# Cached attention decode on one core: K loaded and transposed in pairs of tiles

## The chip, the core and the metric

The kernel runs on one core of a Trainium2 chip. The core has five engines that run their own instruction streams and meet at semaphores: TensorE (PE, with its weight loads shown as PEld), VectorE (DVE), ScalarE (ACT), GpSimd (POOL) and SyncE (SP, which here only issues DMAs). Sixteen DMA engines move data between the device memory and the on-chip memory (SBUF, 128 partitions). The metric is the device time in microseconds of one execution; smaller is better. Before the change the median of three runs is 1311.87 us (1311.55 to 1312.01).

## What is computed

One decode step of a block with grouped-query attention over a long cache, and a gated unit beside it. There are 2 sequences, one new token each, width 512; 32 query heads share 8 key/value heads; the cache holds 32768 positions of 128 numbers per sequence and key/value head. Everything is float32.

```python
xn = _layernorm(x, axis=-1)
# attention
q = (xn @ wq) as 32 heads of 128
scores = einsum("bhqd,bhkd->bhqk", q, k_cache repeated 4 times) * (128 ** -0.5)
o = einsum("bhqk,bhkd->bhqd", softmax(scores), v_cache repeated 4 times)
s = o.reshape(2, 1, 4096) @ wo
# gated unit
gate, up = xn @ W_gate, xn @ W_up
g = silu((relu(gate) * up) @ W_down)
return x + s * g
```

K and V are 268 MB each. Together with `wq`, `wo` and the three matrices of the gated unit the kernel must read 564.7 MB. Each number of K and V is used by the four query heads of one group only.

## The kernel before

**Groups, tiles, steps.** A group is one sequence and one key/value head; there are 16 (`NG`), each with 32768 positions, cut into 4 tiles (`NU`) of 8192 positions (`TK`). A K tile is 4 MiB: 128 partitions x 64 positions x 128 numbers. There are 64 tiles (`NK`). A step `s` of the main loop (line 904) does the scores of tile `s` and, from step 4 on, the softmax weights of tile `s - 4`. At each odd step the values of two tiles, `s - 5` and `s - 4`, follow the scores on PE. Two tiles that share a stretch of 16384 positions are called a pair here: partition `p` holds 128 neighbouring positions of it, tile `2j` the first 64 of these, tile `2j + 1` the others (`rows_of`, line 400). So a tile of K loaded alone takes 32 KB in a row from every 64 KB, and a pair of V takes 64 KB in a row.

**Work of a step.** DVE transposes the K tile in four chunks of 128x2048 numbers, in blocks of 32x32 (`k_transpose`, line 663), from one of two K slots `kslot` into the tiles `kts` (five of them, so that the first chunk of an odd tile has its own). PE multiplies the transposed chunks with the current query `qcur` (`scores`, line 676). DVE copies the scores of the tile before out of PSUM and notes their maximum (`take_scores`), transposes weights (`take_weights`), and between them does the few small operations that a new group needs: at a step divisible by 4 the group's maximum is found, ACT takes the exponentials of its four tiles, and the group before the last is scaled and turned into a column of `ots` (`finish_group`, line 798; its last copy is ACT's). At the group's last step POOL copies the next group's query from `qt` to `qcur` (`take_query`, line 547). `qt` holds every group's query in a form with zeros around it.

**Loads.** All large loads are issued by SP, in program order, and SP waits at each one until the buffer is free. The lists `ahead` and `at` (lines 876 to 897) say at which step each is issued. Before the loop come `wq` (into `wide`), K tiles 0 and 1, then the two matrices of the gated unit (into `wide`, when the query projection has read it). At each step `s` up to 61 K tile `s + 2` is issued into the slot that tile `s` leaves; its wait is for DVE's transposes of tile `s`. At step 1 `W_down` follows, and at each odd step from 3 a pair of V (`load_vv`) goes into `wide`, 64 KB per partition, a single buffer: it waits until PE has done the values of the pair before.

**The end.** The last four V tiles go apart: tiles 60 and 61 one by one into the free K slots (`load_v`), tile 62 whole and tile 63 in two halves into `wide` (`load_apart`). The output weights `wo` come in eight blocks of 1 MiB, one for each key/value head: four into `kts` before the last V (`load_early`), four into a K slot after it (`load_late`), the very last block in three pieces. `project_near` multiplies blocks 0 to 6 with `ots` in one form and `project_far` block 7 in another that is shorter behind the last bytes; `END` is step 68.

**Loops.** DVE and PE run steps 4 to 63 as a hardware loop of 15 rounds of four steps, with semaphore values kept in registers (`looped` and `emit`); ACT, POOL and SP run straight code. `in_halves` shows a tile as two halves of four chunks, eight positions each.

Of the kernel before, what the change touches and what calls it, by code (L numbers as in the profile page):

```python
# [8 lines left out]
P = 128  # L9
Q = 32  # L10
NC = 4
NR = 16
TK = P * NC * NR
EARLY = 4
NEAR = 7
# [147 lines left out]
def decode_block_kernel(nc, x, kc, vc, wq, wo, wg, wu, wd, out):  # L163
# [17 lines left out]
    def sbuf(name, *shape, align=32):  # L181
        return nc.alloc_sbuf_tensor(name, list(shape), F32, align_bytes=align)[:]
# [23 lines left out]
    qd = sbuf("qd", P, REP, B, HKV)  # L206
    qt = sbuf("qt", P, B, HKV, 4, Q)
    qcur = sbuf("qcur", P, 4, Q)
# [20 lines left out]
    def dve(fn, r=(), w=()):  # L229
        pg.op("DVE", fn, r, w)  # L230
# [7 lines left out]
    def load(dst, src, sem, r=(), w=(), engine="SP"):  # L238
        pg.op(engine, lambda e: e.dma_start(dst, src), r, w, dma=sem)  # L239
# [54 lines left out]
    dve(lambda e: e.memset(zero, 0.0), w=["zero"])  # L294
    dve(lambda e: e.memset(qt, 0.0), w=["qt"])
    dve(lambda e: e.memset(heads, 0.0), w=["heads"])
# [99 lines left out]

    def load_k(t):
        load(kslot[t % 2], rows_of(kc, t, 1), f"k{t % 2}", w=[f"k{t % 2}"])

    def rows_of(src, t, n):  # L400
        b, hk = group(t // NU)
        lo = (t % NU) // 2 * 2 * TK
        rows = src[b, hk, lo : lo + 2 * TK, :]
        if n == 2:
            return rows.rearrange("(p r) d -> p (r d)", p=P)
        return rows.rearrange("(p i r) d -> i p (r d)", i=2, p=P)[t % 2]

    HALF = NC * NR * DH

    def place(t):  # L410
        if t in (NK - 4, NK - 3):
            return kslot[t % 2], [f"k{t % 2}"]
        half = wide[:, t % 2 * HALF : (t % 2 + 1) * HALF]
        return half, [f"wide{t % 2}"]

    def load_v(t):
        load(kslot[t % 2], rows_of(vc, t, 1), f"k{t % 2}", w=[f"k{t % 2}"])

    def load_vv(t):
        load(wide, rows_of(vc, t, 2), "v", w=["wide", "wide0", "wide1"])  # L420

    def load_apart(t):
        load(wide[:, :HALF], rows_of(vc, t, 1), "v_a", w=["wide0"])
        n = HALF // 2
        for h in range(2):
            load(
                wide[:, HALF + h * n : HALF + (h + 1) * n],
                rows_of(vc, t + 1, 1)[:, h * n : (h + 1) * n],
                f"v_b{h}",
                w=["wide1" if h == 0 else "wide1h"],  # L430
            )

    def in_halves(tokens):
        return tokens.rearrange("p (h c r d) -> p h c r d", h=2, c=NC, d=DH)

    wo_early = [kts[hk].rearrange("p (j d) -> p j d", j=4) for hk in range(EARLY)]
    late = HKV - EARLY
    WO, WOK = {}, {}

    def load_early():  # L440
        for hk in range(EARLY):
            WO[hk], WOK[hk] = wo_early[hk], [f"kts{hk}"]
            load(
                kts[hk],
                wo[hk * REP * DH : (hk + 1) * REP * DH, :].rearrange("(p j) d -> p (j d)", j=4),
                f"wo{hk}",
                w=[f"kts{hk}"],
            )

    def load_late():  # L450
        slot = kslot[(NK - 4) % 2]
        key = f"k{(NK - 4) % 2}"
        for hk in range(EARLY, HKV):
            i = hk - EARLY
            dst = slot[:, i * 4 * D : (i + 1) * 4 * D]
            WO[hk] = dst.rearrange("p (j d) -> p j d", j=4)
            here = wo[hk * REP * DH : (hk + 1) * REP * DH, :]
            rows = here.rearrange("(p j) d -> p (j d)", j=4)
            cuts = ((0, 4),) if hk < HKV - 1 else ((0, 2), (2, 3), (3, 4))
            WOK[hk] = {}  # L460
            for lo, hi in cuts:
                name = f"{key}_{hk}_{lo}"
                for j in range(lo, hi):
                    WOK[hk][j] = name
                load(
                    dst[:, lo * D : hi * D],
                    rows[:, lo * D : hi * D],
                    f"wo{hk}_{lo}",
                    r=(),
                    w=[key, name] if (hk, lo) == (EARLY, 0) else [name],  # L470
                )

    def project_q():
# [58 lines left out]
        )  # L532
        for kb in range(4):
            part = slice(Q * kb, Q * kb + Q)
            dve(
                lambda e, kb=kb, part=part: e.tensor_copy(  # L536
                    qt[part, :, :, :, kb * REP : (kb + 1) * REP].rearrange(
                        "p b k e h -> p (b k) e h"
                    ),
                    pq2[part, : 4 * nq].rearrange("p (e h g) -> p g e h", e=4, h=REP),  # L540
                ),
                ["pt1"],
                ["qt"],
            )
        take_query(0)

    def take_query(g):
        b, hk = group(g)
        pg.op("POOL", lambda e: e.tensor_copy(qcur, qt[:, b, hk]), ["qt"], ["qcur"])

# [109 lines left out]
    def turned(t, c):  # L660
        i = NC if c == 0 and t % 2 else c
        return kts[i], f"kts{i}"

    def k_transpose(t, c):
        src = kslot[t % 2]
        dst, key = turned(t, c)
        dve(
            lambda e: e.transpose(  # L668
                dst.rearrange("p (h n) -> p h n", h=2),
                in_halves(src)[:, :, c].rearrange("p h r d -> p h (r d)"),  # L670
            ),
            [f"k{t % 2}"],
            [key],
        )

    def scores(t):
        ps = ps_s[t % 2]

        def one(e, c):
            part = turned(t, c)[0].rearrange("p (r e k) -> p r e k", e=4, k=Q)  # L680
            return mm(ps[Q * c : Q * c + Q, :], qcur[:, e, :], part[:, :, e, :], e == 0, e == 3)
# [71 lines left out]
    def values(t):  # L753
        u = t % NU
        at_, keys = place(t)
# [12 lines left out]
        for h in range(2):  # L768
            held = keys if t < NK - 1 or h == 0 else ["wide1h"]
            pe(chain([one(r) for r in range(8 * h, 8 * h + 8)]), [f"wt{t % 2}", *held], ["o"])  # L770

# [26 lines left out]
    def finish_group(g):  # L798
# [15 lines left out]
        dve(lambda e: e.transpose(ot, ob), ["ob"], ["ot"])  # L814
        act(
            lambda e: e.copy(ots[:, hk, :, b * APART], ot.rearrange("p (j m) -> p j m", j=4)[:, :, 0]),
            ["ot"],
# [6 lines left out]
    def project_near(hks):  # L824
        for hk in hks:
            held = WOK[hk] if isinstance(WOK[hk], list) else [WOK[hk][0]]
            pe(
# [11 lines left out]
                ),  # L839
                [f"ots{hk}", *held],  # L840
                ["s0"],
# [45 lines left out]
    at(ahead, NK - 2, load_v, NK - 4)  # L887
    at(ahead, NK - 1, load_v, NK - 3)
    at(ahead, NK - 1, load_early)
    at(ahead, NK - 1, load_apart, NK - 2)  # L890
    at(ahead, NK + 1, load_late)
    at(extra, NK + 2, project_near, range(EARLY))
    at(extra, 1, mlp_gu, "g", 0)
    at(extra, 1, mlp_gu, "u", 1)
    at(extra, 3, mlp_vector)
    at(extra, 3, mlp_down)
    at(extra, 3, total)

    load_k(0)
    load_k(1)  # L900
    project_q()
    load_gu()

    for s in range(END + 1):
# [18 lines left out]
        if s == END:  # L923
            project_near(range(EARLY, EARLY + 1))
        if done is not None:
# [10 lines left out]
        if s == END:  # L936
            project_near(range(EARLY + 1, NEAR))
            project_far(range(NEAR, HKV))
# [13 lines left out]
    with nc.Block(no_gpsimd_drain=True) as block:  # L952
# [5 lines left out]
        @block.scalar  # L958
        def _(e):
            pg.emit("ACT", e, sems)  # L960

# [45 lines left out]
```

## Time and profile before

| what | value |
|---|---|
| median of 3 runs | 1311.87 us |
| time of the profiled execution | 1311.48 us |
| its span, first to last instruction | 1309.8 us |
| PE busy / DVE busy / ACT busy / POOL busy | 894.4 / 704.4 / 54.7 / 5.4 us |
| bytes moved by DMA | 564.80 MB |
| mean granted PE clock | 0.848 of full |

The profile is of one execution. The page gives busy times, then the span in 40 slices (a digit is the busy share in tenths), the DMA queues with packets, megabytes and the share of the 16 engines' span that the packets took, and the chain of work that ended last, followed back from the last instruction. A line of the chain in order of time has start, duration and what ran. A line of the timeline has start and duration in us, engine, source line, operation, the tiles written and read, the count of instructions merged into it, and in brackets how long the engine had been idle and what released it. L242 and L239 are helper lines through which all matmuls and all loads are recorded, so the tile names tell them apart. SPq is SP issuing a DMA; the load itself runs on after it.

### The profile page before, as it was taken

The page shows a single profiled execution, that of the slowest core. Times are in us where ns is not written, and L with a number is a line of the kernel's source. Part 1 is how long each engine was busy: PE and PEld are TensorE (multiplying, and loading weights), DVE is VectorE, ACT ScalarE, POOL GpSimd, SP SyncE. Part 2 cuts the span into 40 slices and gives each one's busy share as a digit, 9 for nine tenths or more (in the row PEclk, how much of TensorE's full clock was granted, in tenths as well). Part 3 has the DMA queues.
Part 4 walks back from the last instruction along what each step waited for, and adds up shares of the span by engine and source line. Part 5 has one row for each costly group of instructions (what it writes and reads, how often), then busy time and mean ns, then how long its engine had stood idle before and what let it go on. Part 6 is the DMA issues. An engine that isn't in the chain of part 4 may idle for free.

```text
span 1309.8 us, 10858 instructions
## 1 busy us (share of the span) xinstructions
PE 894.4 (68%) x4628; PEld 206.3 (16%) x4628; DVE 704.4 (54%) x646; ACT 54.7 (4%) x150; POOL 5.4 (0%) x22
## 2 busy tenths in 40 slices
PE   3676767677676657766666766767767675776785
PEld 1211111111111111111111111111111111111121
DVE  3676655455665545566454566545466654546611
ACT  0001000000000000000000000000000000000000
POOL 0000000000000000000000000000000000000000
PEclk9788788897878889788788877879887788978788
DMA  9999999999999999999999999999999999999998
GB/s 404 432 433 434 438 441 436 428 426 432 433 439 437 430 426 437 436 434 439 434 430 426 434 433 439 434 434 430 435 433 432 439 436 428 428 432 433 441 423 372
DMA packets 16309, 564.80 MB, mean 431 GB/s; under 512 B 1818, under 2 KB 1834, under 8 KB 2220
## 3 DMA queue, kind: packets, MB, share of 16 engines
q1 hardware_dynamic: 16284, 564.67, 99.8%
q8 instruction: 6, 0.10, 0.0%
q14 instruction: 3, 0.02, 0.0%
q10 hardware_dynamic: 16, 0.01, 0.0%
HBM read 564.67 MB, written 0.00 MB: 431 GB/s over the span
## 4 chain that ended last, share of the span: by engine, by line
DMA 77%; PE 21%; DVE 2%; issue 0%; SPq 0%
DMA w<-in_A_v_cache_dram 70%; PE o L242 18%; DMA k<-in_A_wo_dram 3%; DVE kts L668 2%; DMA k<-in_A_k_cache_dram 2%; DMA w<-in_A_wq_dram 2%; PE m_ps L242 1%; PE s L242 1%; PE pt L242 0%; PE d L242 0%; DVE qt L536 0%; DVE st L692 0%; SPq L239 0%; DVE os L786 0%; DVE gy L869 0%
## 5 line engine op out<-in xcount | busy, mean ns | idle before, releaser
L668 DVE STREAM_TRANSPOSE kts<-k 128x2048 f32<-128x2048 f32 x256 | 577.4, 2285 | 462.7 <-DMA k<-in_A_k_cache_dram 462.7
L242 PE MATMUL s<-kts,qcur 128*32 128x512 f32 x2048 | 486.2, 699 | 199.6 <-DVE kts L668 199.6
L242 PE MATMUL o<-w,wt 128*16 128x512 f32 x1984 | 242.1, 638 | 79.1 <-DMA w<-in_A_v_cache_dram 79.1
L242 PEld LDWEIGHTS s<-kts,qcur 128*32 128x32 f32 x2048 | 87.5, 124 | 600.8 <-DVE kts L668 413.5
L242 PEld LDWEIGHTS o<-w,wt 128*16 128x16 f32 x1984 | 56.2, 101 | 247.9 <-issue 148.0
L736 ACT ACTIVATE st<-st,nb 128x512 f32<-128x512 f32 x64 | 45.4, 710 | 1109.7 <-DVE nb L733 1109.7
L242 PE MATMUL pt<-st,perm 128*128 128x512 f32 x128 | 84.5, 749 | 0.0
L692 DVE TENSOR_SCALAR_CACHE_REDUCE st<-s 128x512 f32<-128x512 f32 x64 | 43.0, 672 | 46.8 <-PE s L242 46.8
L707 PE MATMUL m_ps<-ident,mcol 128*1 128x128 f32 x16 | 5.5, 345 | 74.5 <-DVE mcol L706 74.5
L751 DVE STREAM_TRANSPOSE wt<-pt 128x512 f32<-128x512 f32 x64 | 43.3, 676 | 15.0 <-PE pt L242 15.0
L242 PE MATMUL m_ps<-os,heads 128*128 128x512 f32 x34 | 34.1, 1106 | 0.0
L242 PEld LDWEIGHTS pt<-st,perm 128*128 128x128 f32 x128 | 24.7, 222 | 57.9 <-issue 46.6
L242 PE MATMUL m_ps<-negone,mrow 1*128 1x1 f32 x32 | 9.1, 351 | 33.2 <-DVE mrow L722 33.2
L242 PE MATMUL m_ps<-w,wt 128*32 128x512 f32 (+1 forms) x128 | 16.5, 649 | 7.9 <-DMA w<-in_A_wq_dram 7.9
L786 DVE SCALAR_TENSOR_TENSOR os<-o,rl,own 128x512 f32<-128x512 f32 x17 | 12.8, 750 | 12.5 <-PE o L242 10.9
L707 PEld LDWEIGHTS m_ps<-ident,mcol 128*1 128x1 f32 x16 | 1.3, 80 | 88.4 <-DVE mcol L706 88.4
L242 PEld LDWEIGHTS m_ps<-negone,mrow 1*128 1x128 f32 x32 | 7.7, 298 | 37.5 <-DVE mrow L722 37.5
L784 DVE RECIPROCAL rl<-m_ps 128x1 f32<-128x1 f32 x17 | 2.8, 163 | 19.8 <-PE m_ps L242 19.8
L806 DVE TENSOR_REDUCE ob<-m_ps 128x128 f32<-128x512 f32 x17 | 11.2, 658 | 3.0 <-PE m_ps L242 3.0
L736 ACT ACTIVATION_READ_ACCUMULATOR st<-st,nb 128x1 f32 x64 | 12.0, 187 | 0.0
L382 PE MATMUL m_ps<-ident,st 32*128 32x32 f32 x4 | 0.7, 306 | 14.2 <-DVE st L371 14.2
L498 DVE COPY os<-m_ps 128x512 f32<-128x512 f32 x2 | 1.4, 690 | 16.4 <-PE m_ps L242 16.4
(81 smaller groups left out, 114.9 us busy)
## 6 DMA issues: line engine op xcount, KB each, us to landing
k<-in_A_k_cache_dram SPq DMA_DIRECT2D x64, 4096.0 KB, 26.1
k<-in_A_v_cache_dram SPq DMA_DIRECT2D x2, 4096.0 KB, 27.6
kts<-in_A_wo_dram SPq DMA_DIRECT2D x4, 1024.0 KB, 28.8
w<-in_A_v_cache_dram SPq DMA_DIRECT2D x1, 4096.0 KB, 33.4
w<-in_A_v_cache_dram SPq DMA_DIRECT2D x2, 2048.0 KB, 36.7
w<-in_B_W_gate_dram SPq DMA_DIRECT2D x1, 3584.0 KB, 19.3
w<-in_B_W_up_dram SPq DMA_DIRECT2D x1, 3584.0 KB, 27.4
w<-in_B_W_down_dram SPq DMA_DIRECT2D x1, 3584.0 KB, 18.3
```

The source lines that it names most:

```text
L242: return lambda e: e.matmul(out_, lhs, rhs, start=start, stop=stop, skip_group_check=True)
L382: lambda e, k=k: e.transpose(px[:, k * 32 : (k + 1) * 32], xquad[:, k, :], ident[:32, :32])
L498: dve(lambda e, q=qs, h=half: e.tensor_copy(q, pq[h]), [f"m{half}"], [f"os{half}"])
L668: lambda e: e.transpose(dst.rearrange("p (h n) -> p h n", h=2), in_halves(src)[:, :, c].rearrange("p h r d -> p h (r d)"),),
L692: lambda e: e.tensor_scalar(st[u], ps_s[t % 2], SCALE, None, op0=ALU.mult, op1=ALU.max, accum_out=mx[:, u : u + 1],),
L707: pe(lambda e: e.transpose(ps_m[0][:1, :P], mcol, ident), ["mcol", "ident"], ["m0"])
L736: lambda e, u=u: e.activation(st[u], st[u], AF.Exp, bias=nb, scale=1.0, accum_out=ls[:, u : u + 1]),
L751: dve(lambda e: e.transpose(wt[t % 2], ps_p[t % 2]), [f"pt{t % 2}"], [f"wt{t % 2}"])
L784: dve(lambda e: e.reciprocal(rl, ps_m[0][:, :1]), ["m0"], ["rl"])
L786: lambda e: e.scalar_tensor_tensor(os_[0].rearrange("p (c d) -> p c d", c=NC), o_ps.rearrange("p (c d) -> p c d", c=NC), rl, own.unsqueeze ...
L806: lambda e: e.reduce_sum(ob.rearrange("p (j q) -> p q j", j=4), ps_m[1].rearrange("p (c q j) -> p q j c", c=NC, j=4), axis=AX.X,),
```

## The change

- **K in pairs.** `kslot` (two tiles of 32 KB per partition) becomes `kbuf` (two pairs of 64 KB per partition). `load_kk(j)` loads tiles `2j` and `2j + 1` with one DMA of 8 MiB. It is issued at odd steps, pair `j + 2` when the scores of pair `j` are done, behind the V pair of that step.
- **In place.** `kts` goes away; `k_transpose` writes each chunk over itself and `scores` reads it there, in two halves of eight positions.
- **The end.** V tiles 60 and 61 come as one pair into `kbuf[0]`, 62 and 63 as one pair into `wide`; all eight blocks of `wo` follow them into `kbuf[1]`.
- **Order.** K pair 1 is issued behind the gated unit's two matrices, no longer ahead of them; `mlp_vector` moves from step 3 to step 1 and `mlp_down` from step 3 to step 2.
- **Query.** `qt` with its zeros becomes `qall` without; `take_query` multiplies it with a 0/1 mask `block_of` on POOL. Four DVE copies become one.
- **Engines.** The last copy of `finish_group` moves from ACT to POOL. ACT runs steps 4 to 63 as a loop too. The values of a tile are one chain on PE in place of two. A scratch area of the DMA software is set to 2048 bytes.

```diff
-    kslot = [sbuf(f"k{i}", P, NC * NR * DH, align=ALIGN) for i in range(2)]
+    kbuf = [sbuf(f"k{i}", P, 2 * NC * NR * DH, align=ALIGN) for i in range(2)]
     wide = sbuf("w", P, 2 * NC * NR * DH, align=ALIGN)
-    kts = [sbuf(f"kts{c}", P, NR * P, align=ALIGN) for c in range(NC + 1)]
...
-    def load_k(t):
-        load(kslot[t % 2], rows_of(kc, t, 1), f"k{t % 2}", w=[f"k{t % 2}"])
+    def k_keys(b):
+        return [f"k{b}"] + [f"k{b}_{i}_{c}" for i in range(2) for c in range(NC)]
+
+    def load_kk(j):
+        b = j % 2
+        load(kbuf[b], rows_of(kc, 2 * j), f"k{b}", w=k_keys(b))
...
+    def load_vv(j):
+        if 2 * j == NK - 4:
+            load(kbuf[0], rows_of(vc, 2 * j), "k0", w=k_keys(0))
+        else:
+            load(wide, rows_of(vc, 2 * j), "v", w=["wide"])
...
     def take_query(g):
         b, hk = group(g)
-        pg.op("POOL", lambda e: e.tensor_copy(qcur, qt[:, b, hk]), ["qt"], ["qcur"])
+        pg.op(
+            "POOL",
+            lambda e: e.tensor_tensor(
+                qcur.rearrange("p e (k h) -> p e k h", h=REP),
+                qall[:, b, hk].unsqueeze(2).to_broadcast([P, 4, Q // REP, REP]),
+                block_of.rearrange("p (k h) -> p k h", h=REP)
+                .unsqueeze(1)
+                .to_broadcast([P, 4, Q // REP, REP]),
+                op=ALU.mult,
+            ),
+            ["qall", "block_of"],
+            ["qcur"],
+        )
...
     def turned(t, c):
-        i = NC if c == 0 and t % 2 else c
-        return kts[i], f"kts{i}"
+        b, i = t // 2 % 2, t % 2
+        return in_halves(half_of(kbuf[b], t))[:, :, c], f"k{b}_{i}_{c}"
 
     def k_transpose(t, c):
...
+        at_, key = turned(t, c)
+        at_ = at_.rearrange("p h r d -> p h (r d)")
+        dve(lambda e: e.transpose(at_, at_), [f"k{t // 2 % 2}"], [key])
...
-    for s in range(NK - 2):
-        at(ahead, s, load_k, s + 2)
-        if s == 1:
+    for s in range(1, NK, 2):
+        j = s // 2
+        if j == 0:
             at(ahead, s, load_d)
-        if s % 2 and s >= 3:
-            at(ahead, s, load_vv, s - 3)
...
+        elif j < NU // 2 * NG - 1:
+            at(ahead, s, load_vv, j - 1)
+        if j + 2 < NK // 2:
+            at(ahead, s, load_kk, j + 2)
+    at(ahead, NK - 3, load_vv, NK // 2 - 2)
+    at(ahead, NK - 1, load_vv, NK // 2 - 1)
+    at(ahead, NK - 1, load_wo)
...
-    load_k(0)
-    load_k(1)
+    load_kk(0)
     project_q()
     load_gu()
+    load_kk(1)
...
-            pg.emit("ACT", e, sems)
+            pg.emit("ACT", e, sems, loop=(NU, NK))
```

More of the change, by code (lines that the diff above doesn't have):

```diff
@@ L13 @@
 TK = P * NC * NR
-EARLY = 4
 NEAR = 7
@@ L294, in decode_block_kernel @@
     dve(lambda e: e.memset(zero, 0.0), w=["zero"])
-    dve(lambda e: e.memset(qt, 0.0), w=["qt"])
+    dve(lambda e: e.memset(block_of, 0.0), w=["block_of"])
+    for kb in range(4):
+        dve(
+            lambda e, kb=kb: e.memset(block_of[Q * kb : Q * kb + Q, kb * REP : (kb + 1) * REP], 1.0),
+            w=["block_of"],
+        )
     dve(lambda e: e.memset(heads, 0.0), w=["heads"])
@@ L408, in decode_block_kernel, with half_of @@
     HALF = NC * NR * DH
+    def half_of(buf, t):
+        return buf[:, t % 2 * HALF : (t % 2 + 1) * HALF]
     def place(t):
         if t in (NK - 4, NK - 3):
[L412 to L431, printed above, removed]
+            return half_of(kbuf[0], t), "k0"
+        return half_of(wide, t), "wide"
+    def load_vv(j):
[3 more added lines that the diff above has]
+            load(wide, rows_of(vc, 2 * j), "v", w=["wide"])
@@ L450, in load_late, with load_wo @@
[L450 to L455, printed above, removed]
+    def load_wo():
+        for hk in range(HKV):
+            dst = kbuf[1][:, hk * 4 * D : (hk + 1) * 4 * D]
             WO[hk] = dst.rearrange("p (j d) -> p j d", j=4)
@@ L532, in project_q @@
         )
[L533 to L544, printed above, removed]
+        dve(
+            lambda e: e.tensor_copy(
+                qall.rearrange("p b k e h -> p (b k) e h"),
+                pq2[:, : 4 * nq].rearrange("p (e h g) -> p g e h", e=4, h=REP),
+            ),
+            ["pt1"],
+            ["qall"],
+        )
         take_query(0)
@@ L754, in values @@
         u = t % NU
-        at_, keys = place(t)
+        at_, key = place(t)
         w = wt[t % 2].rearrange("p (r m) -> p r m", m=Q)
@@ L766, in one @@
             )
-        for h in range(2):
-            held = keys if t < NK - 1 or h == 0 else ["wide1h"]
-            pe(chain([one(r) for r in range(8 * h, 8 * h + 8)]), [f"wt{t % 2}", *held], ["o"])
+        pe(chain([one(r) for r in range(NR)]), [f"wt{t % 2}", key], ["o"])
     def total():
@@ L814, in finish_group @@
         dve(lambda e: e.transpose(ot, ob), ["ob"], ["ot"])
-        act(
-            lambda e: e.copy(ots[:, hk, :, b * APART], ot.rearrange("p (j m) -> p j m", j=4)[:, :, 0]),
+        pg.op(
+            "POOL",
+            lambda e: e.tensor_copy(ots[:, hk, :, b * APART], ot.rearrange("p (j m) -> p j m", j=4)[:, :, 0]),
             ["ot"],
@@ L839, in project_near @@
                 ),
-                [f"ots{hk}", *held],
+                [f"ots{hk}", WOK[hk][0]],
                 ["s0"],
```

61 lines of the change are left out of this document (16 added, 45 removed).

## The prediction

> **What bounds the kernel now.** I read the page first: the slices, the DMA queues, then the chain that ended last.
>
> ```profile
> span 1309.8 us, 10858 instructions
> DMA  9999999999999999999999999999999999999998
> GB/s 404 432 433 434 438 441 436 428 426 432 433 439 437 430 426 437 436 434 439 434 430 426 434 433 439 434 434 430 435 433 432 439 436 428 428 432 433 441 423 372
> q1 hardware_dynamic: 16284, 564.67, 99.8%
> DMA 77%; PE 21%; DVE 2%; issue 0%; SPq 0%
> ```
>
> One queue, SP's, fills all 16 DMA engines for 99.8% of the span, and no slice falls below nine tenths before the last. The time is the time of 564.67 MB passing through, plus a short head and tail. The chain's 21% of PE misleads: it runs through the values matmuls because the next V load waits for them, but other bytes flow meanwhile. The chain in order of time, two pairs of tiles:
>
> ```profile
> 1101.26 31.08 DMA w<-in_A_v_cache_dram
> 1132.34 0.04 issue
> 1132.38 7.11 PE o L242 x64
> 1139.50 31.54 DMA w<-in_A_v_cache_dram
> ```
>
> A V pair is 8 MiB. It lands 31.5 us after its issue although 8 MiB take some 19.3 us (from V landing to V landing, 1132.34 to 1139.50 + 31.54, pass 38.70 us, for 8 MiB of V and 8 of K). So it stood about 12 us in the queue behind K. That 12 us is the slack of the design; the change can gain only where bytes get cheaper, and lose only where the queue runs empty.
>
> **Gain: fewer packets.** One packet is one partition's row. The trace has no row for a packet, so I take a packet's fixed cost from landings of equal bytes in different packets. K now comes as 128 rows of 32 KB for each 4 MiB tile; the early output weights come as 128 rows of 8 KB for each MiB. In the timeline, a DVE transpose released by K and two PE groups released by weights:
>
> ```profile
> 1142.03 2.31 DVE L668 STREAM_TRANSPOSE kts<-k 128x2048 f32<-128x2048 f32 x1 [14.20 <-DMA k<-in_A_k_cache_dram]
> ...
> 1275.17 1.07 PE L242 MATMUL s<-kts,ots 128*32 128x512 f32 x8 [0.74 <-DMA kts<-in_A_wo_dram]
> 1277.63 1.06 PE L242 MATMUL s<-kts,ots 128*32 128x512 f32 x8 [1.39 <-DMA kts<-in_A_wo_dram]
> ```
>
> A K tile follows the V that landed at 1132.34 and lands at about 1142.01: 9.67 us for 4 MiB, 2.418 us a MiB, at 2 packets per engine and MiB. The weights take 1277.63 - 1275.17 = 2.46 us a MiB, at 8 packets. Six packets more cost 0.042 us: 7 ns each. The change sends a K pair as 8 packets per engine in place of 16: 0.057 us a pair, 1.8 us for 32 pairs. The V of tiles 60 and 61 loses 8 packets per engine, that of 62 and 63 (now 8 of 32 KB and 16 of 16 KB) loses 16: 24 x 7 ns = 0.17 us. Sum **-2.0 us**. A reading error of 0.03 us in the 2.46 moves a packet between 2 and 12 ns and the sum between -0.6 and -3.4 us; I take the middle, since 2.46 rests on one difference. That a 64 KB row goes as one packet shows in the count: 30 V pairs x 128 rows, with the other loads' rows and 16 small packets for each of 113 loads, give 16,272 of the queue's 16,284; rows cut in two would add 3,840.
>
> The Trainium skill, page "DMA: Bandwidth & Descriptors", section "Anatomy of one DMA", gives a fixed cost of about 2.0 us per DMA (fitted on the GpSimd path). Charged for each of the 35 K and V loads that go away it would save 70 us; the 9.67 us above leave no room for that in a full queue, so by the trace the sum stays as it is.
>
> **What could be lost: the slack.** Now a V load at the end of an odd step is followed by a 4 MiB K load at every step, each waiting only for DVE's transposes of its slot. After the change the order on SP's queue is, at the end of each odd step, V pair, then K pair. The V waits for the values matmuls of this step (one buffer, `wide`), the K behind it waits for the step's scores. While a step pair runs, the engines move the 16 MiB issued one pair earlier: V first (19.3 us), then K, until 38.7 us after the pair's own K landed. The next V must be issued before that, by as much as a start takes. So I measure, from the start of a pair's first transpose, when its values end. A pair that opens a group:
>
> ```profile
> 1103.39 2.31 DVE L668 STREAM_TRANSPOSE kts<-k 128x2048 f32<-128x2048 f32 x1 [16.89 <-DMA k<-in_A_k_cache_dram]
> ...
> 1127.29 3.62 PE L242 MATMUL s<-kts,qcur 128*32 128x512 f32 x26 [1.15 <-DVE kts L668]
> 1132.38 7.06 PE L242 MATMUL o<-w,wt 128*16 128x512 f32 x64 [1.47 <-DMA w<-in_A_v_cache_dram]
> 1139.50 0.33 SPq L239 DMA_DIRECT2D w<-in_A_v_cache_dram  x1
> ```
>
> Scores end at 1130.91, 27.5 us after the start. Then PE now waits for V; after the change V has landed at +19.3 and the values run at once: issue at 27.5 + 7.1 + 0.1 = **+34.7**. A pair inside a group, the last of the trace:
>
> ```profile
> 1219.43 2.31 DVE L668 STREAM_TRANSPOSE kts<-k 128x2048 f32<-128x2048 f32 x1 [14.51 <-DMA k<-in_A_k_cache_dram]
> ...
> 1241.79 4.12 PE L242 MATMUL s<-kts,qcur 128*32 128x512 f32 x26 [0.28 <-DVE kts L668]
> ...
> 1248.42 5.32 PE L242 MATMUL o<-w,wt 128*16 128x512 f32 x32 [2.52 <-DMA w<-in_A_v_cache_dram]
> ...
> 1253.99 3.63 PE L242 MATMUL o<-w,wt 128*16 128x512 f32 x32
> ```
>
> Scores at +26.5, values 9.2 us: **+35.7** at worst. The start of a load into an empty queue is bounded by the first load:
>
> ```profile
> 0.74 21.91 DMA w<-in_A_wq_dram
> ```
>
> 21.91 - 19.3 = 2.6 us from issue to landing beyond the transfer; the lead lies between 0 (all of it is the end of a load) and 2.6 us. So the deadline is +36.1 to +38.7. Margin by the strict end: 1.4 us (opening pair) and 0.4 us (inside). I cost the bubble at **0**, from the strict end, keeping the loss for the first rival.
>
> The PE clock decides how thin this is; the busy table by stretch has the clock as its third number from the end:
>
> ```profile
> 1123.00:1132.40 9.40, 5.63 (x33) 1.10 (x35) 4.83 (x3) 0.00 (x0) 0.00 (x0) 1.00 0.97 422
> 1142.00:1152.00 10.00, 5.89 (x10) 0.70 (x14) 9.97 (x7) 0.00 (x0) 0.00 (x0) 0.66 1.02 442
> 1162.60:1171.00 8.40, 6.15 (x26) 1.29 (x26) 0.60 (x2) 0.00 (x0) 0.29 (x1) 0.69 0.93 402
> ```
>
> It is 1.00 in the opening pair's last stretch and falls to 0.66 and 0.69 after pauses. The Trainium skill, "TensorE: Matmul & The Clock Gate", "Part 1: The HAM clock gate", says that an idle window of about 3.4 us halves the clock and a busy one restores it. By that rule the pause between scores and values goes away and values run at 7.1, not 9.2 us, so the inside pairs gain 2 us of margin; but a stretch of transposes, where PE works half the time, may lose it, and the rule leaves that open.
>
> **The other edits, at about nothing.** In-place transposes have the same shape and duration (2.31 us and after); should strides cost 0.1 us each, a pair is 0.8 us longer, still inside the opening margin. The score matmuls read rows in two halves, same element count: 0 to a few percent of 3.62 us. POOL now multiplies in `take_query` and copies to `ots` in place of ACT:
>
> ```profile
> 1168.83 0.29 POOL L549 COPY qcur<-qt 128x128 f32<-128x128 f32 x1 [77.31 <-PE s L242]
> ```
>
> The query is next needed once the next pair's K has landed, 38.7 us after 1142.03, 12 us later, so anything between 0.3 and 2 us for it hides there; the last `ots` copy, between 0 and 0.3 us more, is needed only by the last weights. If those covers were gone: 1.7 us x 15, and 0.3 us once. ACT's loop adds register work before waits: 0 to 0.2 us of the opening pair's margin, where its exponentials lie. At the head, the first K pair lands at 22.65 + 19.3 = 42.0, where transposes start at 38.28 now:
>
> ```profile
> 38.28 11.08 DVE L668 STREAM_TRANSPOSE kts<-k 128x2048 f32<-128x2048 f32 x5
> 69.67 0.33 SPq L239 DMA_DIRECT2D w<-in_B_W_down_dram  x1
> 79.52 2.31 DVE L668 STREAM_TRANSPOSE kts<-k 128x2048 f32<-128x2048 f32 x1 [0.23 <-DMA k<-in_A_k_cache_dram]
> ```
>
> `wd` is issued 31.4 us after the start, so at 73.4; the bytes ahead of it, the same as now, are through at 79.5: 6 us of lead. Its waiting holds K pair 2 behind it on SP, which needs less. Step 4, the first opening pair, follows the moved MLP closely and may start 1 to 3 us late on `take_scores`: one bubble of 0 to 1 us, taken as **+0.2**. Behind the last V pair come 8 MiB of weights instead of 4 (19.7 us), and PE needs 9.2 + 0.75 (scaling) + 1.13 (heads) + 6 x 1.07 + 0.69 + 0.43 = 18.6 us after it; the last groups wait for their weights as now. Both durations are in these rows, from the end:
>
> ```profile
> 1300.55 0.75 DVE L786 SCALAR_TENSOR_TENSOR os<-o,rl,own 128x512 f32<-128x512 f32 x1 [7.45 <-PE o L242]
> 1301.53 1.13 PE L242 MATMUL m_ps<-os,heads 128*128 128x512 f32 x2
> 1304.44 1.07 PE L242 MATMUL s<-k,ots 128*32 128x512 f32 x8 [0.79 <-DMA k<-in_A_wo_dram]
> 1305.58 0.69 DVE L844 COPY os<-s 128x512 f32<-128x512 f32 x1 [1.77 <-PE s L242]
> 1306.32 0.43 PE L242 MATMUL s<-os,fold 128*32 128x128 f32 x8
> ```
>
> Cost 0, up to +1 us at a lower clock.
>
> **Sum.** Profiled execution 1311.48 us, its span 1309.8: -2.0 + 0.2 = 1309.7. The median of the runs, 1311.87, is 0.4 above the profiled one, so the forecast is **1310.1**.
>
> **Rivals.** *Late V* (slower): in opening pairs the clock falls during the sparse transposes; the 26 last score matmuls take 6.15 us, as in the stretch from 1162.60 above. The issue moves from +34.7 to +37.2, past +36.1, and the engines stand for 1.1 us in each of 15 opening pairs: +16 - 2 = **1326**; with 0.3 us each, 1314.5. It decides from an issue later than +36.1. For it: a margin of 1.4 us. Against: the opening pair shown has clock 1.00, and the 2.6 us are the strict end.
> *Cheap packets* (faster): 12 ns a packet, -3.4 us: **1308.5**. For it: the error of 0.03 us.
> *Tail late*: the 18.6 us stretch past 19.7 at a low clock, +1 to +3 us: **1312**.
> *Nothing changes*: 64 KB rows split, 1311.9; the packet count speaks against it.
>
> **Numbers.** Forecast 0.46, late V 0.25, cheap packets 0.19, tail 0.08, nothing 0.02. A measurement of this kernel can tell about 0.2% (2.6 us) from no change: faster means under 1309.25, slower over 1314.5. The forecast's own range, 1309.3 to 1311.3, is "same"; so are tail and nothing; cheap packets go to "faster" with some of the forecast's edge (0.24 in all), late V to "slower" (0.25), same 0.51. The range, 1308.2 to 1317, takes in the packets' far end and the milder part of late V; beyond it I leave 0.16 above and 0.04 below. The likeliest case's own range stands above.
>
> **What would show it.** Right: about 5,000 fewer packets (4,096 rows of K, 384 of V, 16 for each of 35 loads), DMA at nine tenths in every slice but the last, V loads issued 33 to 36 us after their pair's first transpose, PE's values no longer waiting for V inside the loop. Wrong: GB/s slices under 420 in a period of two pairs, DVE waiting for K longer than about 15 us in alternate pairs, or a last weight landing that PE does not wait for.

## The result and the profile after

| | before | after |
|---|---|---|
| median, 7 runs each | 1311.82 us (1311.50 to 1312.01) | 1319.82 us (1318.32 to 1327.87) |
| time of the profiled execution / its span | 1311.48 / 1309.8 us | 1324.54 / 1322.9 us |
| packets of SP's queue | 16,284 | 11,244 |
| mean granted PE clock | 0.848 | 0.827 |

The changed kernel is slower by 0.8%: ratio 1.0079, 95% interval 1.0055 to 1.0103. Its runs also lie 9.5 us apart, where those of before lie within 0.5 us. The page after (span, DMA rows of the slices, the queue, the chain by engine, the groups of the K transposes and of the values, and the issues of V: median us from issue to landing last):

```profile
span 1322.9 us, 10839 instructions
...
DMA  9999999999999999999999999999999999999998
GB/s 412 441 421 423 431 426 428 430 438 418 436 420 442 420 438 438 418 440 410 440 418 434 420 436 422 436 424 440 416 444 424 432 444 432 424 442 438 416 415 352
...
q1 hardware_dynamic: 11244, 564.67, 99.4%
...
DMA 58%; PE 20%; DVE 16%; issue 5%; SPq 1%; DVEq 0%
...
L655 DVE STREAM_TRANSPOSE k<-k 128x2048 f32<-128x2048 f32 x256 | 577.4, 2285 | 474.0 <-DMA k<-in_A_k_cache_dram 474.0
...
L241 PE MATMUL o<-w,wt 128*16 128x512 f32 x1984 | 248.2, 596 | 10.2 <-DMA w<-in_A_v_cache_dram 10.2
...
w<-in_A_v_cache_dram SPq DMA_DIRECT2D x31, 24.6
```

The packets are gone (5,040 of them) and the values no longer wait for V (10.2 us in all). The row of digits says that nothing is wrong, since a slice of 33 us still rounds to nine tenths when 2 us of it are lost. The loss is in the row below it: slices of 410 to 424 alternate with slices near 440. And V now lands 24.6 us after its issue. A pair of V takes 19.3 us, so it stood about 5 us in the queue, where the chain of before had 12. The timeline shows where the rest of the loss lies. Two pairs of tiles (first transposes, scores, values, SP's issues), the first of them opening a group:

```profile
576.83 2.31 DVE L655 STREAM_TRANSPOSE k<-k 128x2048 f32<-128x2048 f32 x1 [18.62 <-DMA k<-in_A_k_cache_dram]
587.07 1.28 ACT L717 ACT_TABLE_LOAD   x1
...
600.49 4.87 PE L241 MATMUL s<-k,qcur 128*32 128x512 f32 x25 [1.15 <-DVE k L655]
...
605.21 7.46 PE L241 MATMUL o<-w,wt 128*16 128x512 f32 x61
...
612.70 0.33 SPq L238 DMA_DIRECT2D w<-in_A_v_cache_dram  x1
613.07 0.43 SPq L238 DMA_DIRECT2D k<-in_A_k_cache_dram  x1
615.66 2.31 DVE L655 STREAM_TRANSPOSE k<-k 128x2048 f32<-128x2048 f32 x1 [14.62 <-DMA k<-in_A_k_cache_dram]
...
647.23 0.33 SPq L238 DMA_DIRECT2D w<-in_A_v_cache_dram  x1
647.60 0.43 SPq L238 DMA_DIRECT2D k<-in_A_k_cache_dram  x1
656.65 2.31 DVE L655 STREAM_TRANSPOSE k<-k 128x2048 f32<-128x2048 f32 x1 [19.82 <-DMA k<-in_A_k_cache_dram]
```

DVE has nothing else to do when a pair starts, so the start of its first transpose is the landing of that pair's K where the row names that DMA. From 576.83 to 615.66 pass 38.8 us; V is issued at 612.70, 35.9 us after the pair's start and 2.96 us before the landing of the K ahead of it, the last load in the queue. The V and the K behind it then take until 656.65: 40.99 us where 38.64 is usual. So 2.35 us were lost although the V was issued before the queue was empty.

For the whole loop stand the first transposes of pair 2 and pair 31. The timeline of the kernel before (pair 31's row, 1219.43, stands in the prediction; at pair 2 DVE comes from a copy, so its K may have landed some tenths earlier):

```profile
97.24 0.69 DVE L637 COPY os<-d 128x512 f32<-128x512 f32 x1 [3.73 <-PE d L242]
97.85 2.30 DVE L668 STREAM_TRANSPOSE kts<-k 128x2048 f32<-128x2048 f32 x1
```

And that of the kernel after:

```profile
107.96 2.31 DVE L655 STREAM_TRANSPOSE k<-k 128x2048 f32<-128x2048 f32 x1 [2.27 <-DMA k<-in_A_k_cache_dram]
...
1240.83 2.31 DVE L655 STREAM_TRANSPOSE k<-k 128x2048 f32<-128x2048 f32 x1 [14.96 <-DMA k<-in_A_k_cache_dram]
```

From pair 2 to pair 31 the kernel before needs 1219.43 - 97.85 = 1121.6 us and the one after 1240.83 - 107.96 = 1132.9 us, so 11.3 of the 13.1 us by which the spans differ arise in these 29 pairs. (In the changed kernel a pair starts when both tiles are there, some 9.7 us later in the stream; with that taken off, about 0.4 us arise ahead of pair 2 and 1.4 us behind the start of pair 31.)

### The profile page after: what moved, and what is told of

Its sections match the earlier page's. It is cut to its first block, busy times and chain, and to the rows that moved or that the text cites. A ratio compares the mean times of both kernels' runs of the same rounds, so it can differ in the third digit from the quotient of the medians.

```text
span 1322.9 us, 10839 instructions
## 1 busy us (share of the span) xinstructions
PE 874.5 (66%) x4628; PEld 203.8 (15%) x4628; DVE 701.9 (53%) x647; ACT 69.4 (5%) x147; POOL 10.5 (1%) x39
## 3 DMA queue, kind: packets, MB, share of 16 engines
q1 hardware_dynamic: 11244, 564.67, 99.4%
## 4 chain that ended last, share of the span: by engine, by line
DMA 58%; PE 20%; DVE 16%; issue 5%; SPq 1%; DVEq 0%
DMA k<-in_A_k_cache_dram 54%; DVE k L655 15%; PE s L241 11%; PE o L241 8%; DMA k<-in_A_wo_dram 3%; DMA w<-in_A_wq_dram 2%; PE m_ps L241 1%; DVE st L673 1%; SPq L238 1%; PE d L241 0%; DVEq L150 0%; DVEq L143 0%; DVE gy L848 0%; DVE gy L850 0%; DVEq L141 0%
## 5 line engine op out<-in xcount | busy, mean ns | idle before, releaser
L655 DVE STREAM_TRANSPOSE k<-k 128x2048 f32<-128x2048 f32 x256 | 577.4, 2285 | 474.0 <-DMA k<-in_A_k_cache_dram 474.0
L241 PE MATMUL s<-k,qcur 128*32 128x512 f32 x2048 | 496.3, 714 | 229.8 <-DVE k L655 229.7
L241 PE MATMUL o<-w,wt 128*16 128x512 f32 x1984 | 248.2, 596 | 10.2 <-DMA w<-in_A_v_cache_dram 10.2
L241 PEld LDWEIGHTS s<-k,qcur 128*32 128x32 f32 x2048 | 88.9, 125 | 637.2 <-DVE k L655 445.2
L717 ACT ACTIVATE st<-st,nb 128x512 f32<-128x512 f32 x64 | 45.4, 711 | 1116.7 <-DVE nb L714 1116.7
L241 PEld LDWEIGHTS o<-w,wt 128*16 128x16 f32 x1984 | 60.3, 97 | 158.9 <-issue 158.6
L241 PE MATMUL pt<-st,perm 128*128 128x512 f32 x128 | 81.7, 728 | 0.0
L527 POOL TENSOR_TENSOR qcur<-qall,block_of 128x128 f32<-128x128 f32 x16 | 6.5, 408 | 862.6 <-PE s L241 828.3
L717 ACT ACTIVATION_READ_ACCUMULATOR st<-st,nb 128x1 f32 x64 | 12.0, 187 | 0.0
## 6 DMA issues: line engine op xcount, KB each, us to landing
w<-in_A_v_cache_dram SPq DMA_DIRECT2D x31, 24.6
```

The costliest lines, as they stand in the source:

```text
L241: return lambda e: e.matmul(out_, lhs, rhs, start=start, stop=stop, skip_group_check=True)
L527: lambda e: e.tensor_tensor(qcur.rearrange("p e (k h) -> p e k h", h=REP), qall[:, b, hk].unsqueeze(2).to_broadcast([P, 4, Q // REP, REP]) ...
L655: dve(lambda e: e.transpose(at_, at_), [f"k{t // 2 % 2}"], [key])
L717: lambda e, u=u: e.activation(st[u], st[u], AF.Exp, bias=nb, scale=1.0, accum_out=ls[:, u : u + 1]),
```

## Experiments

Two theories stood first. *Late V*: V is issued too late, so DMA engines run dry. *Long rows*: 64 KB rows, or transposes in place, slow the stream itself. Beside these stood the loop on ACT, which loads an activation table in every round (`L717 ACT ACT_TABLE_LOAD`, 15 of 1.28 us).

**1. K ahead of V.** The two loads of an odd step change places on SP.

```diff
-        elif j < NU // 2 * NG - 1:
-            at(ahead, s, load_vv, j - 1)
         if j + 2 < NK // 2:
             at(ahead, s, load_kk, j + 2)
+        if 0 < j < NU // 2 * NG - 1:
+            at(ahead, s, load_vv, j - 1)
```

> The changed kernel with one edit: at each odd step from 3 on, SP issues the K pair ahead of the V pair. Late V (each V load is issued too short a time before the engines run dry): K waits only for the scores, some 7 us earlier than V, and V is then queued behind a K pair that still has to run, so both loads are issued 8 us or more before the queue is empty; the loss goes away and the packets' gain shows: 1309.5 to 1311 us, K pair to K pair 38.65 us throughout. Long rows (64 KB rows, or transposes in place beside the loads, slow the engines): order does not matter, 1318 to 1326 us. ACT and POOL edits: they lengthen the opening pairs, which matters only while the V lead is short, so on this theory alone 1318 to 1326 us too.

Measured: 1339.08 us (1335.01 to 1341.96), ratio 1.0200 (1.0181 to 1.0218). I had expected a gain and overlooked what the exchange makes late. The timeline of this kernel, an opening pair:

```profile
590.24 0.17 DVE L763 RECIPROCAL rl<-m_ps 128x1 f32<-128x1 f32 x1 [2.89 <-PE o L241]
...
617.28 0.33 SPq L238 DMA_DIRECT2D k<-in_A_k_cache_dram  x1
618.56 0.13 PEld L241 LDWEIGHTS o<-w,wt 128*16 128x16 f32 x8 [2.22 <-DMA w<-in_A_v_cache_dram]
```

Now the values of a pair run in the middle of the next one, DVE waits for them before it can scale a group, its transposes end later, and K is issued 1.28 us before the V ahead of it lands at 618.56. At the end of the kernel it is worse: V pair after V pair, each waiting for the values of the one before.

```profile
1244.56 8.59 PE L241 MATMUL o<-w,wt 128*16 128x512 f32 x64 [4.12 <-DMA w<-in_A_v_cache_dram]
...
1253.22 0.33 SPq L238 DMA_DIRECT2D w<-in_A_v_cache_dram  x1
...
1275.03 0.15 PEld L241 LDWEIGHTS o<-w,wt 128*16 128x16 f32 x8 [7.04 <-DMA w<-in_A_v_cache_dram]
```

Two V pairs land 30.5 us apart there (1244.56 and 1275.03) instead of 19.3, since the second is issued 8.7 us behind the landing of the first, into an empty queue: 11 us are lost in this one place. The run removes V's lateness only to make others; it doesn't tell the theories apart.

**2. ACT straight.** The loop on ACT is undone.

```diff
-            pg.emit("ACT", e, sems, loop=(NU, NK))
+            pg.emit("ACT", e, sems)
```

> The changed kernel with ACT running straight code again instead of its loop. Late V: the opening pairs' scores ended 27.3 to 29.0 us after the first transpose with the loop, as before it; nothing to win, 1317 to 1328 us like the changed kernel. ACT edits: the 15 table loads of 1.28 us that the loop has brought in and its register work go away, 15 times 0.5 to 1.3 us: 1306 to 1314 us. Long rows: as the changed kernel.

Measured: 1322.72 us (1316.59 to 1328.34), ratio 1.0098 (1.0079 to 1.0118). No gain: all four runs lie above the 1306 to 1314 us that the theory of the ACT edits gave, so the table loads don't make the loss, and that theory falls. (A cost of 1 or 2 us would be lost in the 12 us between these runs.) (The load at 587.07 above runs when the group's exponentials are done; ACT then has tens of us of rest.)

**3. Rows of 32 KB.** A K pair comes as two DMAs of 128 rows of 32 KB; every transpose still waits for both.

```diff
-        return [f"k{b}"] + [f"k{b}_{i}_{c}" for i in range(2) for c in range(NC)]
+        return [f"k{b}", f"k{b}h0", f"k{b}h1"] + [f"k{b}_{i}_{c}" for i in range(2) for c in range(NC)]
...
-        load(kbuf[b], rows_of(kc, 2 * j), f"k{b}", w=k_keys(b))
+        for i in range(2):
+            cut = slice(i * HALF, (i + 1) * HALF)
+            held = [f"k{b}h{i}"] + [f"k{b}_{i}_{c}" for c in range(NC)]
+            load(kbuf[b][:, cut], rows_of(kc, 2 * j)[:, cut], f"k{b}h{i}", w=held)
...
-        dve(lambda e: e.transpose(at_, at_), [f"k{t // 2 % 2}"], [key])
+        dve(lambda e: e.transpose(at_, at_), [f"k{t // 2 % 2}h{i}" for i in range(2)], [key])
```

> The changed kernel with each K pair loaded by two DMAs of 4 MiB, rows of 32 KB as before the change; the transposes of a pair still wait for both halves, so that all waits stay. Late V: the same short lead, 1.4 to 1.8 us more for the packets: 1319 to 1330 us. Long rows: the engines are as fast as before the change, 1310 to 1313 us.

Measured: 1318.72 us (1312.77 to 1323.99), ratio 1.0049 (1.0029 to 1.0068). Still slow and as spread as the changed kernel, with K's rows as short as before. The median lies just under the 1319 to 1330 us of late V; of the ten runs two (1312.77 and 1312.86) lie in the range of long rows. So short rows alone don't bring the old time back. The other half of that theory, transposes in place, is untouched here; experiments 4 and 5 settle both.

**4. The same two DMAs, each half waited for by itself.** Only the transposes' waits differ from experiment 3.

```diff
-        dve(lambda e: e.transpose(at_, at_), [f"k{t // 2 % 2}h{i}" for i in range(2)], [key])
+        dve(lambda e: e.transpose(at_, at_), [f"k{t // 2 % 2}h{t % 2}"], [key])
```

> The changed kernel with each K pair loaded by two DMAs of one tile, rows of 32 KB, and the transposes of a tile waiting for their own half alone, so that a pair starts 9.7 us earlier against the engines. Late V: the V load is issued 9 us earlier, no loss, but the packets' gain is given back: 1311 to 1312.5 us. Long rows: as fast as before, 1311 to 1312.5 us. ACT and POOL edits: 1318 to 1326 us. Together with the run of 32 KB rows whose transposes wait for both halves it parts the row's length from the time of the start.

Measured: 1311.59 us (1311.49 to 1313.32), ratio 1.0001 (0.9992 to 1.0010). The timeline of this kernel, from one pair to the next but one:

```profile
562.33 2.31 DVE L658 STREAM_TRANSPOSE k<-k 128x2048 f32<-128x2048 f32 x1 [15.49 <-DMA k<-in_A_k_cache_dram]
...
598.51 0.33 SPq L238 DMA_DIRECT2D w<-in_A_v_cache_dram  x1
...
601.03 2.31 DVE L658 STREAM_TRANSPOSE k<-k 128x2048 f32<-128x2048 f32 x1 [14.49 <-DMA k<-in_A_k_cache_dram]
...
639.72 2.31 DVE L658 STREAM_TRANSPOSE k<-k 128x2048 f32<-128x2048 f32 x1 [16.64 <-DMA k<-in_A_k_cache_dram]
```

V is again issued 36.2 us after the pair's start. But 601.03 is the landing of a first half; the second half, 9.67 us of the stream, is still behind it, so V has 12.2 us of lead and the distances are 38.70 and 38.69 us. Same loads, same bytes, same in-place transposes as in experiment 3, and the loss is gone: what costs is waiting for the second half, which puts all of PE's work, and with it the issue of V, 9.67 us later in the stream.

**5. Values ahead of scores.** 64 KB rows and whole pairs, as changed; at odd steps PE does the values before the step's scores, so V is issued earlier.

```diff
             k_transpose(s, 3)
-            scores(s)
-        if s % NU == NU - 1 and s + 1 < NK:
-            take_query(s // NU + 1)
         if 0 <= w < NK:
             take_weights(w)
...
                 values(v)
+        if s < NK:
+            scores(s)
+        if s % NU == NU - 1 and s + 1 < NK:
+            take_query(s // NU + 1)
...
```

> The changed kernel with one edit in the order of PE's work: at an odd step the values of the two tiles come ahead of the step's scores, not behind them; loads, rows of 64 KB, transposes in place and the ACT loop stay. Late V: the values can start when V has landed, 19.3 us after the pair's K, and end some 8 us later, so V is issued about 28 us after the pair's start in place of 34 to 36, with 9 to 11 us until the next K pair has landed; the engines never stand and the packets' gain shows: 1309.5 to 1311 us. Long rows: the rows are the same, 1316 to 1328 us. ACT and POOL edits: the same edits, 1316 to 1328 us.

Measured: 1310.57 us (1310.09 to 1311.74, 11 runs) beside 1311.68 (1311.48 to 1312.32, 20 runs) for before; ratio 0.9992 (0.9983 to 1.0001). The timeline of this kernel:

```profile
185.02 2.31 DVE L655 STREAM_TRANSPOSE k<-k 128x2048 f32<-128x2048 f32 x1 [17.60 <-DMA k<-in_A_k_cache_dram]
...
209.22 3.63 PE L241 MATMUL o<-w,wt 128*16 128x512 f32 x32 [1.17 <-DVE wt L732]
212.66 3.62 PE L241 MATMUL s<-k,qcur 128*32 128x512 f32 x32
...
212.91 0.33 SPq L238 DMA_DIRECT2D w<-in_A_v_cache_dram  x1
...
223.62 2.31 DVE L655 STREAM_TRANSPOSE k<-k 128x2048 f32<-128x2048 f32 x1 [14.46 <-DMA k<-in_A_k_cache_dram]
...
262.21 2.31 DVE L655 STREAM_TRANSPOSE k<-k 128x2048 f32<-128x2048 f32 x1 [16.91 <-DMA k<-in_A_k_cache_dram]
```

V leaves 27.9 us after the pair's start, 10.7 us before the K ahead of it lands, and the pairs are 38.60 and 38.59 us apart. PE's clock is lower than in the changed kernel (0.790 against 0.827 in the profiled executions) and PE's values wait for V again (102.6 us in all, against 10.2), without any cost. The 9 us of loss are gone by the order of PE's work alone, with rows of 64 KB and transposes in place: long rows fall. What remains is a gain of 1.1 us, at the edge of the noise, since the interval just takes in no change.

**6. Values longer.** Eight idle matmuls behind the values of each odd tile, in the changed kernel's order; they write to a bank that nothing reads, so V is issued later and nothing else changes.

```diff
+        more = [
+            mm(ps_d[32 * c : 32 * c + 32, :], ident[:, :32], at_[:, c * 512 : (c + 1) * 512], True, True)
+            for n in range(2)
+            for c in range(4)
+        ]
-        pe(chain([one(r) for r in range(NR)]), [f"wt{t % 2}", key], ["o"])
+        pe(chain([one(r) for r in range(NR)] + (more if t % 2 else [])), [f"wt{t % 2}", key], ["o"])
```

> The changed kernel with eight more matmuls at the end of each odd step's values chain, which read the V buffer and write a PSUM bank that is free; the output is the reference's. Each V load is issued some 1.8 us later. Late V: every opening pair loses 1.8 us more, a pair inside a group, with a lead of 3 to 9 us now, loses 0 to 1.8: 15 x 1.8 to 30 x 1.8 on 1320, so 1347 to 1375 us. Long rows, and ACT and POOL edits: PE has some 10 us to spare in a pair, nothing changes, 1316 to 1328 us.

Measured: 1339.78 us (1337.23 to 1342.09), ratio 1.0207 (1.0191 to 1.0223): 20 us over the changed kernel, in the direction expected, by less than expected. The timeline of this kernel, an opening pair and the pair inside the group behind it:

```profile
266.44 2.31 DVE L655 STREAM_TRANSPOSE k<-k 128x2048 f32<-128x2048 f32 x1 [18.10 <-DMA k<-in_A_k_cache_dram]
...
302.54 0.33 SPq L238 DMA_DIRECT2D w<-in_A_v_cache_dram  x1
...
305.26 2.31 DVE L655 STREAM_TRANSPOSE k<-k 128x2048 f32<-128x2048 f32 x1 [14.42 <-DMA k<-in_A_k_cache_dram]
...
337.29 1.90 PE L241 MATMUL d<-w,ident 128*32 128x512 f32 x16
...
339.25 0.33 SPq L238 DMA_DIRECT2D w<-in_A_v_cache_dram  x1
...
346.61 2.31 DVE L655 STREAM_TRANSPOSE k<-k 128x2048 f32<-128x2048 f32 x1 [20.18 <-DMA k<-in_A_k_cache_dram]
```

The eight extra matmuls are the 16 records at 337.29, two for each. The lead of the V at 302.54 is 2.7 us, and the next distance is 346.61 - 305.26 = 41.35 us. The late issue makes its own reprieve: that lengthened stretch gives the V of the next pair (339.25) 7.4 us of lead, so mostly only every second pair pays (the opening ones: here they lose 0.3 to 2.9 us, those inside a group at most 0.4). My expectation charged more of them.

**7. Both.** Values first, with the same eight idle matmuls.

> The kernel with the values ahead of the scores, and in it the same eight extra matmuls behind the values of each odd step that cost the changed kernel some 20 us; the output is the reference's. Late V: the V loads there have 9 to 11 us from issue until the K pair before them has landed, and need some 4.5; 1.8 us less leaves 7 to 9, so the extra matmuls cost nothing: 1310 to 1311.5 us, K pair to K pair 38.64 us. If the extra matmuls cost by themselves (PE as the bound, or its reads beside the loads), 1325 to 1340 us here too.

Measured: 1311.12 us (1310.44 to 1312.16), ratio 0.9998 (0.9989 to 1.0007). The matmuls that cost 20 us in experiment 6 cost 0.6 us here (1311.12 against 1310.57), where the leads are 7.1 to 9.6 us. So it is the time of V's issue that the loss follows, not the amount of work on PE.

**How early is early enough.** Lead of a V load (from its issue to the start of the next pair's first transpose) against the distance from that start to the next one, less 38.62 us, for the 28 or 27 inner pairs of the changed kernel and of experiments 2, 5, 6 and 7, from the rows of their timelines as read above:

```
lead, us     loads   mean loss, us   least to most
under 2          4            1.6     1.5 to 1.8
2 to 3          15            1.8    0.05 to 2.9
3 to 4           7            0.5    0.06 to 1.1
4 to 5          30            0.2       0 to 1.1
5 to 6          14            0.06      0 to 0.2
6 and more      69            0.05      0 to 0.7
```

Below 3 us the loss does not follow the lead closely: in the changed kernel 2.96 us cost 2.4 us and 2.81 us cost 0.05.

In the profiled execution of the changed kernel these losses sum to 11.9 us, 10.8 of them behind V loads of opening pairs (leads 2.8 to 4.8 us) and 1.1 behind those of inside pairs (leads 4.5 to 9.4).

**Standing engines or longer packets.** The traces also hold the start and the duration of every packet, which the views don't list. Between 107 and 1230 us of the span, per DMA engine in the mean of the 16: how long an engine has no packet under way, and by how much its 64 KB packets together exceed the 2.418 us of their median:

```
kernel                          standing, us   longer packets, us
changed                                  2.0                  9.2
values first (exp. 5)                    0.1                  0.1
values longer (exp. 6)                  18.4                 11.5
```

So in the changed kernel "run dry" is the smaller part. A V issued late mostly makes packets last longer: 251 of the 301 packets of over 2.5 us start within 8 us of a V issue that had less than 5 us of lead, the longest taking 4.4 us. The pages agree: the queue's packets take 99.4% of 1322.9 us in the changed kernel, 1315 us, and 99.7% of 1309.0 us, 1305 us, with values first, for the same bytes in the same rows. That is why the busy shares hide the loss. In experiment 6, with shorter leads, standing is the larger part. Why a packet lasts longer behind a late issue no run shows.

## Why the prediction failed

**Where V would be issued: right.** The prediction had +34.7 us for opening pairs and +35.7 at worst for inside ones. The timeline has +34.2 to +35.9 and +31.6 to +34.3. That the values would follow the scores without a pause at full clock was right too; where an opening pair is at its latest, the sparse transposes had lowered the clock to 0.66 for the last scores, as the late V rival has it. The busy table of the changed kernel for the opening pair above, clock third from the end:

```profile
600.40:605.40 5.00, 4.91 (x32) 1.25 (x36) 0.64 (x2) 0.00 (x0) 0.00 (x0) 0.66 0.97 419
605.40:612.70 7.30, 7.30 (x63) 1.69 (x55) 0.00 (x0) 0.00 (x0) 0.00 (x0) 1.00 1.00 431
```

**How early it must be issued: the step that failed.** The prediction took the lead that a load needs as 0 to 2.6 us, put the deadline at +36.1 to +38.7, and costed the bubble at 0 "from the strict end". Its 2.6 us came from the first load, 21.91 - 19.3 us, into a queue where all 16 engines stood ready. In the loop they do not end a load together. The trace's semaphore records, in which each of the 16 engines reports its part of a load, say for the loads around 612.70 (us of the span, the last part of the K pair set to its landing at 615.66):

```
K pair ahead of the V issued at 612.70: first part 613.80, last 615.66
that V pair:                            first part 634.50, last 637.31
difference:                                        20.70,      21.65   (19.3 with lead enough)
```

The first engine reported its last part 1.1 us after V's issue. Counted from there, 2.6 us of start make the first part 1.5 us late; it is 1.4. What these 2.6 us are shows in the packets of the V that experiment 1 issued into an empty queue at 1253.22: the first start 0.95 us behind the issue, all but one of the first 16 take 3.0 to 3.3 us in place of 2.42, the others 2.42, and the load lands 21.8 us behind its issue, 2.5 more than 19.3. Over the trace of the changed kernel the first and the last engine end a load 0.8 to 3.1 us apart, in the median 2.2; with values first it is mostly 1.6. So, as an estimate, the need is 2.6 us and the spread, 4.2 to 4.8 us before the landing, which is where the losses of the table begin. The deadline was at about +34, not +36.1, and opening pairs were behind it every time. What the prediction left out of its deadline is this spread, and it thought of standing engines alone, where most of the loss is longer packets. The last part lost more than the first (2.3 us): by the packet rows, the engine that reported it began its first packet of the V 3.8 us behind the issue and took 3.5 us for it. Why it came so late stays open, since the rows don't name the engines.

The Trainium skill, page "DMA: Bandwidth & Descriptors", section "Anatomy of one DMA — SWDGE (gpsimd) path", gives about 2.0 us of fixed cost for a DMA, most of it the confirmation of the last byte. Taken as the lead needed, it would have let the V at 612.70 through with 2.96 us; the 40.99 us measured behind it do not agree with that use of it.

**The price of the late V rival: about right in sum, in part by luck.** It was given 1.1 us in each of 15 opening pairs (1326 us), or 0.3 us (1314.5), deciding from an issue later than +36.1. The place, and a V issued too late, were right. But no V was issued later than +35.9, so by the rival's own deadline nothing would have been lost: the low clock delayed the issues by less than it said, and the loss began nearly 2 us earlier. The opening pairs lost 0 to 2.4 us each, 0.8 in the mean of 14 in the profiled execution, which ended at 1324.5; for the median run at 1319.8 the estimate is half a microsecond (11.9 us less the 4.7 between the two runs, over 14).

**Fewer packets: right in kind, half the size.** Forecast -2.0 us at 7 ns a packet, between -0.6 and -3.4. With the bubble away (experiment 5) the median is 1.1 us under before, 1310.57 against 1311.68: about 4 ns for each of the 280 packets per engine that the prediction counted. The single difference of 0.042 us on which the 7 ns rested was too large. The trace does have rows for packets, against what the prediction says: inside the loop of the kernel before, packets of 32 KB follow each other on an engine every 1.209 us and those of 64 KB every 2.414 us (medians), so two of 32 KB take 0.004 us more, 4 ns for the extra packet. Experiment 4, which sends K in 32 KB rows (15,852 packets) and also leaves no bubble, ends at 1311.59, 1.0 us above experiment 5; the two differ in PE's order too, so this only supports the size.

**Head, tail and the other edits: about nothing, as costed.** In the timeline of experiment 5 the first and the last pair of the loop are

```profile
107.58 2.31 DVE L655 STREAM_TRANSPOSE k<-k 128x2048 f32<-128x2048 f32 x1 [1.16 <-DMA k<-in_A_k_cache_dram]
...
1228.11 2.31 DVE L655 STREAM_TRANSPOSE k<-k 128x2048 f32<-128x2048 f32 x1 [14.46 <-DMA k<-in_A_k_cache_dram]
```

so pair 2 starts within 0.1 us of before's 97.85 + 9.67, the loop takes 1120.5 us (1.1 less than before), and the end of the span, 1309.0, lies 80.9 us behind, 0.2 us more than before's 1309.8 - 1219.43 - 9.67. In-place transposes took 2285 ns in the mean. POOL's product for the query and its copy to `ots`:

```profile
L527 POOL TENSOR_TENSOR qcur<-qall,block_of 128x128 f32<-128x128 f32 x16 | 6.5, 408 | 862.6 <-PE s L241 828.3 <-DVE qall L514 34.3
...
L796 POOL COPY ots<-ot 128x4 f32<-128x4 f32 x17 | 3.3, 193 | 439.1 <-DVE ot L793 439.1
```

Both durations are inside their bounds (0.3 to 2 us, and up to 0.3 us more than ACT's).

**The signs.** Right: packets, issue times, values that don't wait. "DMA at nine tenths" held and showed nothing, as 11 us spread over 40 slices can't change a digit. Of the signs of being wrong, GB/s slices under 420 that alternate are what the page after shows. DVE's waits for K over 15 us in alternate pairs came too (18.62 and 19.82), but experiment 5 has 17.60 and 16.91 without a loss, so that sign tells nothing.

## What to carry to other kernels

Where one queue sets the time, measure how long each load stands in the queue before its own bytes move (issue to landing, less its transfer). A change that makes consumers wait for a larger load takes that load's extra transfer (here 9.67 us) out of this stand. In this kernel next to nothing was lost where 5 us or more remained (0.06 us in the mean), between 4 and 5 us a load lost up to 1.1 us, below 4 us between 0.05 and 2.9, and the run times scattered. Compare the summed packet times too: a busy share near 100% also counts packets that last longer than they need. Before giving the larger load up, look for work that frees the buffer and can run earlier: putting the values ahead of the scores turned +8 us into -1.1.

## What was not expected of the hardware

- Issuing a load before the queue is empty is not enough: with 2.96 us of lead 2.35 us were lost. The 16 engines end a load 0.8 to 3.1 us apart, and the first packets of a late load take up to 4.4 us in place of 2.42.
- ACT's loop brought 15 table loads of 1.28 us at the line of the exponentials, one for each round, where the straight code of before and of experiment 2 has a single one; here they lay in ACT's rest, and taking them out gained nothing.
- With some 10 us of lead the stream takes 38.59 to 38.68 us for 27 of 28 pairs (38.77 for the other) at a PE clock of 0.79, so that clock does not reach it. With 3 us the same stream varies from run to run by 9.5 us (1318.32 to 1327.87). What shifts a run from one end to the other was not tried.
